# Two lists of loads and steps, and the last sum of an attention and feed-forward kernel, in a new order

## The chip, the cores and the metric

The kernel runs on one core of a Trainium2 chip. The metric is the device time of one execution in microseconds (us), the median of several runs. TensorE (PE) does the matmuls, ScalarE (ACT) and VectorE (DVE) the elementwise work, GpSimd (POOL) a little of it, and SyncE (SP) issues nearly all DMAs, one after the other, in an order that the program fixes.

## What is computed

The reference first does two small attentions between x (8 x 8 heads x 512 x 64) and a state (8 x 8 heads x 32 x 64), and feeds the joined result (4352 rows of 512) through a layer with a squared ReLU:

```python
xread = softmax(scale * x @ state.T) @ state
sread = softmax(scale * state @ x.T) @ x
rows = concatenate([xread, sread], axis=2)      # 8 x 8 heads x 544 x 64 -> 4352 x 512
h = maximum(rows @ w_in, 0.0)                   # d_ff = 2048
out = (h * h) @ w_out                           # 4352 x 512
```

## The kernel before, in words

The rows of `out` are worked on in nine blocks: blocks 0 to 7 hold the 512 rows that one batch entry's x reads make, block 8 the 256 rows of all state reads. Each f32 operand of a large matmul is split into a high and a low part in a faster format (`k_hi`, `k_lo`; `g_hi`, `g_lo`; the two halves of `w`), and three matmuls (high by high, high by low, low by high) stand for one. All matmuls of a block go through line 414 (`mm3`).

Rows @ w_in is not taken from the reads themselves: state @ w_in is made once per block ("W2", tile `w`) and multiplied by the softmax weights (`k_hi`, `k_lo`). For blocks 0 to 3 W2 is made on the spot (`w2ps`). For blocks 4 to 7 it is made beforehand by `quad_w2` (line 855), for four blocks at a time: ACT copies a piece of w_in (`q`, L860), DVE takes the low part (L863), PE multiplies (`qps`, L868), the result is copied out of PSUM (`qo`, L872) and SP writes it to HBM (`w_d`, L875). `load_w2` (L879) reads it back in four loads of 512 KB per block (tile `w2r`, L881), and `split_w2` splits each (ACT L887, DVE L890).

In the late blocks 4 to 8 the second product is done on pairs of d_ff slices, p = 0 to 7. For a pair, seven products of smaller matrices take the place of eight (the "fewer" tiles hold sums of w_out's quarters). A late block has two halves u: the first 256 rows are summed while the hidden slices are made, pair by pair, and the second 256 rows afterwards, in the order of `again_order`, which this text calls places 0 to 7. For a pair the ACT lines are 1086 (ReLU), 1087 (square of the first half's rows, into `ga`) and 1089 (square of the second half's rows, into `gb`). Most `gb` tiles are written to HBM at once (`g_d`, L1091), with their sums (`ge`, L1149), and read back later into `ga` and `gd` (L1094, L1104), since SBUF is full. A `gb` tile comes from a pool tag "g" with two buffers, one of which is held by a kept pair; so the next `gb` waits until the write of the last one has landed. The hidden slice is held in PSUM (tile `ph`, two buffers): PE can't start the slice after the next before ACT has read both squares out of it.

For each pair's operands ACT makes the high parts (L1138, L1142) and DVE the low parts (L1139, L1143). Even places use the tiles `k_hi` and `k_lo`, odd ones a tile `gs` from the tag "x", which has two buffers. The same tag holds `xn` (x by rows, loaded by `load_n`, L503) and `xp` (x cut into 32 x 32 pieces for a transpose on DVE, loaded by `load_p`, L519, four steps of four DMAs of 64 KB; the transposes are the steps `prep`, L544). The tag "wraw", also with two buffers, holds `w2r`, `eB` (exponentials on their way to HBM, written by the step `transposes` as `e_d`, L729) and `eT` (read back by `load_e`, L733, for the state read `sread`).

The order of all work is written out by hand as a list of words. A word is a step; a `~` in front runs it up to its next yield, so that its parts land between those of other steps. Each engine and SP keep exactly this order. The list for blocks 0 to 3 is the string `FIRST`; for the late blocks the function `late` builds it. In `late`, `a[p]` are the words after pair p in the first half of block b and `z[p]` those in the second half (`a[7]` stands at place 1 of the second half), n is block b + 1 and m is b + 2:

```python
        a[0] = "" if b == 4 else f"load_w2.{b}.2"
        a[1] += f" ~w2.{b}.4 w2.{b}.4 load_w2.{b}.3 "
            a[4] += f" {two} load_w2.{n}.0"
            a[7] += f" {two} ~w2.{n}.0 w2.{n}.0 load_w2.{n}.1"
                a[k + 1 + j // 2] += f" load_p.{m}.{j}"
```

Sums are accumulated in PSUM banks x, y, z and w (`acc_x` and so on), and read out by `step_sum` (L1152). At the end of block 8 pair 7 is summed with plain products: six matmuls of 512 columns into y, then six of 256 and three of 512 columns into w; DVE adds y and then w to the partial results in two halves each (L1209), and after each half SP stores it (L1214).

Of the kernel before, what the change touches and what calls it, by code (L numbers as in the profile page):

```python
# [97 lines left out]
    ~quad.0.1 ~accumulate.1.10 ~w2.0.4 ~hidden.1.15 ~transposes.3  # L98
    hidden.1.13 ~w2.0.4 w2.0.4 split_k.0.0 ~split_k.0.1 ~accumulate.1.13 load_p.4.3
    hidden.1.14 accumulate.1.13 split_k.0.1  # L100
    hidden.1.15 ~quad.0.2 ~quad.0.1 accumulate.1.10 accumulate.1.14 ~quad.0.2 ~hidden.0.8 ~hidden.0.8 quad.0.1
    accumulate.1.12
    hidden.0.8 ~quad.0.3 ~softmax.3.0 quad.0.2 ~quad.0.3 load_p.4.1 load_p.4.2 accumulate.1.15 ~hidden.0.9
    ~hidden.0.10 ~hidden.0.9 ~quad.0.3 accumulate.0.8 ~quad.0.3 ~quad.1.0
# [12 lines left out]
    ~sread.3 accumulate.3.0 ~quad_states.1 transposed_scores.4.0 ~exp_s.4.0  # L117
    hidden.3.1 ~hidden.3.2 ~quad_states.1 accumulate.3.1 load_p.5.0 transposed_scores.4.1 ~softmax.4.0 ~hidden.3.2
    ~quad_states.1
    hidden.3.2 ~softmax.4.1 ~exp_s.4.0 ~hidden.3.3 exp_s.4.0 quad_states.1 accumulate.3.2 ~hidden.3.3 ~exp_s.4.1  # L120
    hidden.3.3 ~exp_s.4.1 ~hidden.3.4 exp_s.4.1 ~quad.2.0 ~transposes.4 accumulate.3.3 ~hidden.3.4 ~softmax.4.1
    ~softmax.4.0 ~transposes.4
    hidden.3.4 transposes.4 ~hidden.3.5 ~quad.2.0 accumulate.3.4 ~hidden.3.5 spill_wi.1
    hidden.3.5 ~quad.2.0 ~softmax.4.0 ~hidden.3.6 accumulate.3.5 ~quad.2.0 sread.3 ~softmax.4.0 ~quad.2.1 quad.2.0
    ~hidden.3.6 ~hidden.3.7
    ~fewer.0 ~fewer.0
    hidden.3.6 load_p.5.1 spill_wi.2 ~w2.3.4 ~quad.2.1 load_p.5.3 ~w2.3.4 load_w2.4.0 accumulate.3.6 w2.3.4 ~hidden.3.7 ~quad.2.1
    hidden.3.7 fewer.0 ~hidden.3.8 ~quad.2.2 ~fewer.1 ~quad.2.2 accumulate.3.7 ~hidden.3.8 ~quad.2.1 ~softmax.4.1
    ~fewer.1 hidden.3.8 ~fewer.1 fewer.1 quad.2.1 ~hidden.3.9 ~softmax.4.0 ~softmax.4.0 ~quad.2.2 accumulate.3.8 ~quad.2.3 ~quad.2.2 ~hidden.3.9
    ~quad.2.3 quad.2.2 ~hidden.3.10  # L130
    hidden.3.9 load_p.5.2 ~softmax.4.0 ~quad.2.3 ~hidden.3.10 accumulate.3.9 ~quad.3.0
    hidden.3.10 ~fewer.2 ~fewer.2 ~fewer.2 ~quad.2.3 ~softmax.4.0 ~hidden.3.11 quad.2.3 ~w2.3.6 accumulate.3.10 ~w2.3.6 ~hidden.3.11 w2.3.6
    ~hidden.3.12
# [13 lines left out]
    return p < FEWER[blk][u]  # L147


def again_order(blk):  # L150
    n = FEWER[blk][1]
    if blk == 4:
        return [2, 3, 0, 1, 4, 5, 6, 7]
    return [p + k for p in range(n - 2, -1, -2) for k in (0, 1)] + [0] * (n % 2) + list(range(n, 8))


def late():

    w = []
    for b in (4, 5, 6, 7):  # L160
        n, m, last = b + 1, b + 2, b == 7
        ob = again_order(b)
        more = {u: [""] * 8 for u in range(2)}
        a, z = more[0], more[1]
        two = f"~softmax.{n}.0 ~softmax.{n}.1"
        k = 1
        a[0] = "" if b == 4 else f"load_w2.{b}.2"
        a[k] += f" scores.{n} ~sread.{b} ~sread.{b} "
        a[1] += f" ~w2.{b}.4 w2.{b}.4 load_w2.{b}.3 "
        if last:  # L170
            a[k] += f"~exp_s.{n}.0 ~exp_s.{n}.1 sread.{b} load_n.8.0"
        else:
            a[k] += f"transposed_scores.{n}.0 transposed_scores.{n}.1 ~exp_s.{n}.0 ~exp_s.{n}.1 sread.{b} start.{m}"
        a[k + 1] += f" ~exp_s.{n}.0 ~exp_s.{n}.1 exp_s.{n}.0 exp_s.{n}.1"
        a[3] += f" ~w2.{b}.6 w2.{b}.6"
        a[3 if last else 4] += f" ~transposes.{n} ~transposes.{n} transposes.{n}"
        if last:
            a[3] += " ~move_sread"
            a[4] = "load_e.8"
            z[1] = "~move_sread move_sread load_wi.0 ~sread.8 ~sread.8 sread.8 load_wi.1"  # L180
            z[3] = "~split_wi.0 split_wi.0 load_wi.2"
            z[5] = "~split_wi.1 split_wi.1"
        else:
            a[2] += f" {two}"
            a[3] += f" {two}"
            a[4] += f" {two} load_w2.{n}.0"
            a[5] += f" {two}"
            a[6] += f" {two}"
            a[7] += f" {two} ~w2.{n}.0 w2.{n}.0 load_w2.{n}.1"
            for j in range(4):  # L190
                a[k + 1 + j // 2] += f" load_p.{m}.{j}"
            z[2] += f" {two}"
            z[3] += f" ~softmax.{n}.0 softmax.{n}.0"
            z[4] += f" ~w2.{n}.2 w2.{n}.2 ~softmax.{n}.1 softmax.{n}.1"
            z[5] += f" prep.{m}.0 prep.{m}.1"
            z[6] += f" prep.{m}.2 prep.{m}.3 load_e.{n} load_n.{n}.0"
        if b == 4:
            a[1] += " load_f.4"
            a[4] = a[4].replace(" transposes.5", " load_f.5 transposes.5") + " ~fewer.4"
            a[5] += " fewer.4 ~fewer.5"  # L200
            a[6] += " ~fewer.5 ~fewer.5"
            z[0] += " fewer.5"
            z[7] += " ~fewer.6 ~fewer.6"
        if b == 5:
            a[0] += " fewer.6"
        before = "accumulate.3.15" if b == 4 else f"sum.{b - 1}.1.{again_order(b - 1)[7]}"
        chain = "~hidden.{b}.{f} ~hidden.{b}.{g} {pe} ~hidden.{b}.{f} hidden.{b}.{f} {few} ~hidden.{b}.{g} {few}"
        chain += " ~parts.{b}.0.{q} hidden.{b}.{g} parts.{b}.0.{q}"

        def hide(blk, q, pe):  # L210

            if blk == 8:
                t = "~hidden.{b}.{f} ~hidden.{b}.{g} {pe} hidden.{b}.{f} {few} "
                t += f"~split_wi.{q + 1} split_wi.{q + 1} load_wi.{q + 2} " if q else ""
                t += "hidden.{b}.{g} {few} {out} {few2} parts.{b}.0.{q}"
            else:
                t = chain
            few = "~parts.{b}.0.{q}".format(b=blk, q=q) if seven(blk, q, 0) else ""
            out = f"~sum.8.0.{q - 1}" if q == FEWER[8][0] else ""
            t = t.format(b=blk, f=2 * q, g=2 * q + 1, q=q, pe=pe, out=out, few=few, few2="~parts.{b}.0.{q}".format(b=blk, q=q))  # L220
            return t

        def load(blk, at):

            return f"load_g.{blk}.{ob[at]} load_d.{blk}.{ob[at]}"

        def again(q):

            few = f"~parts.{b}.1.{q} ~parts.{b}.1.{q}" if seven(b, q, 1) else ""
            return f"{few} parts.{b}.1.{q}"  # L230

        if b == 4:
            w += [hide(4, 0, "~" + before), before, "~w2.4.2 w2.4.2 load_w2.4.2"]
        for p in range(8):
            w += [load(b, 3).split()[0]] if p == 6 else []
            if p < 7:
                w += [hide(b, p + 1, f"~sum.{b}.0.{p} " + (before if p == 0 and b > 4 else ""))]
            else:
                w += [f"~sum.{b}.0.{p}", again(ob[0])]
                w += ["sum.{}.0.{}".format(b, 6)] if FEWER[b][0] > 6 else []  # L240
            w += [f"sum.{b}.0.{p}"] if p < (6 if FEWER[b][0] > 6 else 7) else []
            w += [{4: load(b, 2), 6: load(b, 3).split()[1], 7: load(b, 4)}[p]] if p in (4, 6, 7) else []
            w += [a[p]] if p < 7 else []
        for p in range(8):
            if p == 7:
                w += [f"~hidden.{n}.0 ~hidden.{n}.1"]
            w += [f"~sum.{b}.1.{ob[p]}"]
            if p == 1:
                w += [f"sum.{b}.0.7"]
            if p < 7:  # L250
                w += [again(ob[p + 1]), f"sum.{b}.1.{ob[p]}"]
            if p == 7:
                w += [hide(n, 0, "").replace(f"~hidden.{n}.0 ~hidden.{n}.1  ", "")]
            w += [a[7]] if p == 1 else []
            w += [load(b, k) for k in {0: (5, 6), 1: (7,)}.get(p, ())]
            w += [z[p]]
    for p in range(8):
        if p < 7:
            w += [hide(8, p + 1, f"~sum.8.0.{p} " + ("sum.7.1.7" if p == 0 else ""))]
        else:  # L260
            w += ["~sum.8.0.7"]
        w += [f"sum.8.0.{p}"]
    return " ".join(w)
# [35 lines left out]
def tile_attn_moe(  # L299
# [17 lines left out]
    B, H, S, D = x.shape  # L317
    Ns = state.shape[2]
    DM, DFF = w_in.shape
# [17 lines left out]
    V, A, T, SP, PL = nc.vector, nc.scalar, nc.tensor, nc.sync, nc.gpsimd  # L337
    traced, last = [0], {}
# [44 lines left out]
    def banks(name):  # L383

        return ps_b.tile([P, 2, S], F32, tag="psb", name=name)
# [766 lines left out]
    def step_sum(blk, u, p):  # L1152
# [22 lines left out]
        else:  # L1175
            for bank, ws in ((by, (a11, a12)), (bw, (a21, a22))):
                pairs = [(a, (wo[2 * p + k][:, 0], wo[2 * p + k][:, 1])) for k, a in enumerate(ws)]
                if at == n and bank is bw:
                    for h in range(2):
                        c = ts(h, DM // 2)  # L1180
                        mm3(bank[:, c], [(pairs[0][0], [r[:, c] for r in pairs[0][1]])], first=False, last=False)
                    pairs = pairs[1:]
                mm3(bank, pairs, first=False, last=end)
# [19 lines left out]
        if end:  # L1203
            n = P // B
            for i, o, bank in zip((1, 0), held.pop((blk, u, "o")), (by, bw)):
                o = o.rearrange("p h f -> p (h f)")
                halves = [slice(0, DM // 2), slice(DM // 2, DM)]
                for c in [slice(0, DM)] if blk < B else halves:
                    V.tensor_add(o[:, c], bank[:, c], o[:, c])  # L1209
                    if blk < B:  # L1210
                        SP.dma_start(out_v[blk, ts(2 * u + i, P)], o)
                    else:
# [300 lines left out]
```

## Time and profile before

| | us |
|---|---|
| median of 3 runs (640.1 to 641.74) | 641.44 |
| the profiled execution | 639.41 |
| its span, first to last instruction | 637.6 |
| PE busy | 626.7 (98%) |
| DVE busy | 496.5 (78%) |
| ACT busy | 431.3 (68%) |
| POOL busy | 26.2 (4%) |

PE is the engine to look at: 98% of the span it has a matmul in flight. The granted clock is 0.999 of full speed (2.4 GHz) over the span. In the trace the late block 4 lies at about 332 to 393 us, block 5 at 393 to 457, block 6 to 522, block 7 to 587, block 8 to the end. A time in a row of the timeline is the start of the instruction from the span's start; the second number is how long it took, or for a row with a count the time from the first one's start to the last one's end; in brackets stands how long the engine was idle before it, and what ended that.

### The profile page before, as it was taken

How to read it: one execution, taken by the hardware profiler on the slowest of the kernel's cores; microseconds unless marked ns; L12 is line 12 of the kernel's file. 1: busy time of each engine (PE TensorE's matmuls, PEld its weight loads, DVE VectorE, ACT ScalarE, POOL GpSimd, SP SyncE). 2: the span in 40 equal slices, each digit the busy share in tenths (PEclk: the TensorE clock that was granted, in tenths of full speed). 3: DMA queues.
4: the chain of work that ended last, by engine and by line, in shares of the span. 5: the costliest groups of instructions: out<-in, count | busy, mean ns of one | idle time of the engine just before them, and what ended most of it. 6: DMA issues, size and time to landing. Idle time of an engine off the chain costs nothing.

```text
span 637.6 us, 11600 instructions
## 1 busy us (share of the span) xinstructions
PE 626.7 (98%) x4296; PEld 518.6 (81%) x4296; DVE 496.5 (78%) x1001; ACT 431.3 (68%) x813; POOL 26.2 (4%) x37
## 2 busy tenths in 40 slices
PE   7999999999999999999999999999999999999997
PEld 6577777777787777777888788899989998999996
DVE  5999767574676888868987797999769976865996
ACT  5987658754765565778896775777667766875452
POOL 1210000000000000000000202000200020001000
PEclk9999999999999999999999999999999999999999
DMA  8983948450422777196376895669465857694421
GB/s 315 370 189 119 280 104 233 118 132 2 115 87 66 225 191 213 19 213 181 87 229 208 202 233 174 193 153 258 154 217 131 229 175 213 175 269 145 127 73 34
DMA packets 155561, 109.22 MB, mean 171 GB/s; under 512 B 104560, under 2 KB 126576, under 8 KB 155504
## 3 DMA queue, kind: packets, MB, share of 16 engines
q1 hardware_dynamic: 154688, 108.08, 59.6%
q8 instruction: 34, 0.56, 0.4%
q10 hardware_dynamic: 816, 0.39, 0.2%
q14 instruction: 23, 0.19, 0.1%
HBM read 66.83 MB, written 41.62 MB: 170 GB/s over the span
## 4 chain that ended last, share of the span: by engine, by line
PE 84%; ACT 6%; DMA 4%; DVE 4%; issue 1%; SPq 0%; DVEq 0%; ACTq 0%
PE acc L414 25%; PE ph L414 24%; PE acc_x L414 6%; PE acc_z L414 6%; PE acc_yw L414 6%; PE acc_y L414 4%; PE w2ps L426 3%; PE acc_w L414 3%; PE ph L1223 2%; DMA g_d<-gb 2%; PE qps L868 2%; PE pr L745 1%; PE sc L426 1%; PE ph L1224 1%; DMA w2r<-w_d 1%; DMA xn<-in_x_dram 1%
## 5 line engine op out<-in xcount | busy, mean ns | idle before, releaser
L414 PE MATMUL ph<-k_hi,w 128*128 128x512 f32 x504 | 171.8, 395 | 1.6 <-ACT gb L1089 1.6
L414 PE MATMUL acc<-wo,g_hi 128*128 128x512 f32 x512 | 159.3, 392 | 0.1
L414 PEld LDWEIGHTS ph<-k_hi,w 128*128 128x128 f32 x504 | 94.6, 188 | 31.9 <-issue 8.0
L414 PEld LDWEIGHTS acc<-wo,g_hi 128*128 128x128 f32 x512 | 95.5, 188 | 24.7 <-issue 3.3
L414 PE MATMUL acc<-wo,g_lo 128*128 128x512 f32 x256 | 100.1, 391 | 0.4 <-DVE g_lo L998 0.4
L414 PE MATMUL ph<-k_lo,w 128*128 128x512 f32 x252 | 98.3, 390 | 0.0
L998 DVE TENSOR_TENSOR g_lo<-ph,g_hi 128x512 fp32r<-128x512 f32 x64 | 43.7, 685 | 35.6 <-ACT g_hi L407 34.8
L414 PEld LDWEIGHTS acc<-wo,g_lo 128*128 128x128 f32 x256 | 48.0, 188 | 11.9 <-DVE g_lo L998 1.7
L990 ACT ACTIVATE ph<-ph 128x512 f32<-128x512 f32 x59 | 34.6, 587 | 32.2 <-PE ph L414 31.4
L414 PEld LDWEIGHTS ph<-k_lo,w 128*128 128x128 f32 x252 | 47.4, 188 | 8.4
L1086 ACT ACTIVATE ph<-ph 128x512 f32<-128x512 f32 x64 | 37.7, 589 | 19.9 <-PE ph L414 18.3
L991 ACT ACTIVATE ph<-ph 128x512 f32<-128x512 f32 x59 | 34.3, 582 | 1.9
L407 ACT CAST g_hi<-ph 128x512 fp32r<-128x512 f32 x53 | 31.1, 587 | 5.7 <-PE acc L414 2.8
L1138 ACT CAST gs<-ga 128x384 fp32r<-128x384 f32 (+1 forms) x32 | 17.5, 545 | 21.2 <-PE acc_yw L414 13.8
L1138 ACT CAST k_hi<-ga 128x384 fp32r<-128x384 f32 (+1 forms) x40 | 20.9, 522 | 13.2 <-DVE ga L1232 12.7
L1143 DVE TENSOR_TENSOR k_lo<-gd,k_hi 128x512 fp32r<-128x512 f32 x36 | 24.8, 688 | 4.6 <-ACT k_hi L1142 4.6
L1087 ACT ACTIVATE ga<-ph 128x256 f32<-128x256 f32 x64 | 24.6, 385 | 2.0
L1190 POOL TENSOR_TENSOR o_x<-o_x 128x256 f32<-128x256 f32 x5 | 4.7, 930 | 517.2 <-DMA xp<-in_x_dram 300.9
L829 DVE TENSOR_TENSOR w<-w2ps,w 128x512 fp32r<-128x512 f32 (+1 forms) x34 | 20.1, 633 | 7.3 <-ACT w L407 7.3
L407 ACT CAST w<-w2ps 128x512 fp32r<-128x512 f32 (+1 forms) x26 | 13.6, 567 | 17.3 <-DVE w L405 10.3
L1139 DVE TENSOR_TENSOR k_lo<-ga,k_hi 128x384 fp32r<-128x384 f32 (+1 forms) x40 | 22.3, 559 | 3.8 <-ACT k_hi L1138 3.8
L890 DVE TENSOR_TENSOR w<-w2r,w 128x1024 fp32r<-128x1024 f32 x16 | 19.5, 1220 | 6.8 <-ACT w L887 6.7
(236 smaller groups left out, 1380.0 us busy)
## 6 DMA issues: line engine op xcount, KB each, us to landing
w_d<-qo SPq DMA_DIRECT2D x32, 256.0 KB, 2.6
w2r<-w_d SPq DMA_DIRECT2D x16, 512.0 KB, 4.5
wo_raw<-in_moe_w_out_dram SPq DMA_DIRECT2D x16, 511.8 KB, 8.0
wi_raw<-in_moe_w_in_dram SPq DMA_DIRECT2D x16, 511.5 KB, 6.3
xp<-in_x_dram SPq DMA_DIRECT2D x112, 64.0 KB, 2.5
g_d<-gb SPq DMA_DIRECT2D x24, 256.0 KB, 3.3
ga<-g_d SPq DMA_DIRECT2D x24, 256.0 KB, 5.0
g_d<-ge SPq DMA_DIRECT2D x19, 256.0 KB, 2.6
```

Source lines behind the costliest of these rows:

```text
L407: A.copy(out, src)
L414: T.matmul(ps, l, r, start=first and i == 0, stop=last and i == len(seq) - 1)
L426: T.matmul(ps, l, r, start=True, stop=True)
L829: V.tensor_sub(w[:, u, g, 1], ps[g], w[:, u, g, 0].bitcast(F32))
L990: A.activation(ph, ph, AF.Relu)
L991: A.activation(ph, ph, AF.Square)
L998: V.tensor_sub(glo, ph, ghi.bitcast(F32))
L1086: A.activation(ph, ph, AF.Relu)
L1087: A.activation(raws[blk, 0, p][:, 2 * k : 2 * k + 2].rearrange("p i t -> p (i t)"), ph[:, : 2 * P], AF.Square)
L1138: A.copy(hi[:, r], raw[:, r])
L1139: V.tensor_sub(lo[:, r], raw[:, r], hi[:, r].bitcast(F32))
L1143: V.tensor_sub(lo[:, 4:], d, hi[:, 4:].bitcast(F32))
```

## The change

1. `FIRST`, block 1: the rest of `quad.0.1` (copying out of PSUM, DVE L872, and its two writes) goes ahead of `~quad.0.2` (the low part of the next piece, DVE L863) and of two parts of `hidden.0.8`.
2. `FIRST`, block 3: the first part of `exp_s.4.1` (DVE reduce L628 and a small multiply, L630) goes behind the end of `hidden.3.3` (DVE `g_lo`, L998); the first part of `quad.2.0` (ACT copies, L860) goes behind the end of `hidden.3.4`; `load_w2.4.0` is issued after `quad.2.2` and not after `load_p.5.3`.
3. `late`: the first W2 load of block n moves from `a[4]` to `a[3]`, the second from `a[7]` to `a[5]`, the third from `a[0]` of block n to `z[4]` of the block before. The loads of x move from `a[2]` and `a[3]` to `z[2]` and `z[3]`.
4. `step_sum`, block 8: the last sum into w is made as two halves of six matmuls of 256 columns, each half in a bank of its own (`tail` is the second); y's result is added and stored whole, w's in two halves. There are three last stores in place of four.

```diff
-    hidden.1.15 ~quad.0.2 ~quad.0.1 accumulate.1.10 accumulate.1.14 ~quad.0.2 ~hidden.0.8 ~hidden.0.8 quad.0.1
+    hidden.1.15 ~quad.0.2 ~quad.0.1 accumulate.1.10 accumulate.1.14 quad.0.1 ~quad.0.2 ~hidden.0.8 ~hidden.0.8
...
-    hidden.3.2 ~softmax.4.1 ~exp_s.4.0 ~hidden.3.3 exp_s.4.0 quad_states.1 accumulate.3.2 ~hidden.3.3 ~exp_s.4.1
-    hidden.3.3 ~exp_s.4.1 ~hidden.3.4 exp_s.4.1 ~quad.2.0 ~transposes.4 accumulate.3.3 ~hidden.3.4 ~softmax.4.1
+    hidden.3.2 ~softmax.4.1 ~exp_s.4.0 ~hidden.3.3 exp_s.4.0 quad_states.1 accumulate.3.2 ~hidden.3.3
+    hidden.3.3 ~exp_s.4.1 ~exp_s.4.1 ~hidden.3.4 exp_s.4.1 ~transposes.4 accumulate.3.3 ~hidden.3.4 ~softmax.4.1
     ~softmax.4.0 ~transposes.4
-    hidden.3.4 transposes.4 ~hidden.3.5 ~quad.2.0 accumulate.3.4 ~hidden.3.5 spill_wi.1
+    hidden.3.4 ~quad.2.0 transposes.4 ~hidden.3.5 ~quad.2.0 accumulate.3.4 ~hidden.3.5 spill_wi.1
...
-    hidden.3.6 load_p.5.1 spill_wi.2 ~w2.3.4 ~quad.2.1 load_p.5.3 ~w2.3.4 load_w2.4.0 accumulate.3.6 w2.3.4 ~hidden.3.7 ~quad.2.1
+    hidden.3.6 load_p.5.1 spill_wi.2 ~w2.3.4 ~quad.2.1 load_p.5.3 ~w2.3.4 accumulate.3.6 w2.3.4 ~hidden.3.7 ~quad.2.1
...
-    ~quad.2.3 quad.2.2 ~hidden.3.10
+    ~quad.2.3 quad.2.2 load_w2.4.0 ~hidden.3.10
...
+XP = 2, 2, 3, 3
...
-        a[0] = "" if b == 4 else f"load_w2.{b}.2"
+        a[0] = ""
...
-            a[3] += f" {two}"
-            a[4] += f" {two} load_w2.{n}.0"
-            a[5] += f" {two}"
+            a[3] += f" {two} load_w2.{n}.0"
+            a[4] += f" {two}"
+            a[5] += f" {two} load_w2.{n}.1"
             a[6] += f" {two}"
-            a[7] += f" {two} ~w2.{n}.0 w2.{n}.0 load_w2.{n}.1"
-            for j in range(4):
-                a[k + 1 + j // 2] += f" load_p.{m}.{j}"
+            a[7] += f" {two} ~w2.{n}.0 w2.{n}.0"
+            for j, at in enumerate(XP):
+                z[at] += f" load_p.{m}.{j}"
...
-            z[4] += f" ~w2.{n}.2 w2.{n}.2 ~softmax.{n}.1 softmax.{n}.1"
+            z[4] += f" ~w2.{n}.2 w2.{n}.2 ~softmax.{n}.1 softmax.{n}.1 load_w2.{n}.2"
...
+                if blk == B and end and bank is bw:
+                    for h, half in enumerate((bw, tail := banks("acc8_0_v")[:, 0])):
+                        c = ts(h, DM // 2)
+                        mm3(half[:, c], [(a, [r[:, c] for r in rs]) for a, rs in pairs], first=h == 1, last=True)
+                    continue
...
-                for c in [slice(0, DM)] if blk < B else halves:
-                    V.tensor_add(o[:, c], bank[:, c], o[:, c])
+                for c in [slice(0, DM)] if blk < B or i else halves:
+                    V.tensor_add(o[:, c], (tail if c.start else bank)[:, c], o[:, c])
```

## Rows read from the trace of the kernel before

**Rows 1.** Page: engine totals; costliest groups (busy, mean ns, idle before).

```profile
PE 626.7 (98%) x4296; PEld 518.6 (81%) x4296; DVE 496.5 (78%) x1001; ACT 431.3 (68%) x813; POOL 26.2 (4%) x37
...
L414 PE MATMUL acc<-wo,g_hi 128*128 128x512 f32 x512 | 159.3, 392 | 0.1
```

**Rows 2.** Timeline of PE, block 4 (start us, us, instruction, idle before).

```profile
362.58 1.52 PE L414 MATMUL acc_w<-wo,gs 128*128 128x512 f32 x6
365.55 0.50 PE L414 MATMUL ph<-k_hi,w 128*128 128x512 f32 x1 [1.45 <-ACT gb L1089]
...
367.39 0.50 PE L414 MATMUL ph<-k_hi,w 128*128 128x512 f32 x1 [0.17 <-ACT gb L1089]
```

**Rows 3.** Timeline of ACT, block 4.

```profile
359.26 0.38 ACT L1089 ACTIVATE gb<-ph 128x256 f32<-128x256 f32 x1
...
365.11 0.38 ACT L1089 ACTIVATE gb<-ph 128x256 f32<-128x256 f32 x1 [3.53 <-DMA g_d<-gb]
```

**Rows 4.** Timeline of SP, block 4.

```profile
356.98 4.20 SPq L519 DMA_DIRECT2D xp<-in_x_dram  x8
```

**Rows 5.** DMAs issued at 361.28, 407.58, 409.68, 337.99: KB, us to landing.

```profile
g_d<-gb SPq DMA_DIRECT2D x1, 256.0 KB, 3.7
...
w2r<-w_d SPq DMA_DIRECT2D x1, 512.0 KB, 3.7
...
g_d<-gb SPq DMA_DIRECT2D x1, 256.0 KB, 2.3
...
g_d<-gb SPq DMA_DIRECT2D x1, 256.0 KB, 5.4
```

**Rows 6.** Timeline of PE, last place of block 4.

```profile
389.62 0.62 PE L414 MATMUL acc_yw<-wo,k_hi 128*128 128x512 f32 x2
390.29 0.50 PE L414 MATMUL acc_yw<-wo,k_lo 128*128 128x512 f32 x1
```

**Rows 7.** Timeline of ACT, second half of block 4.

```profile
386.72 1.05 ACT L887 CAST w<-w2r 128x1024 fp32r<-128x1024 f32 x1 [0.80 <-DMA w2r<-w_d]
```

**Rows 8.** DMAs issued at 434.29 and 437.75 (block 5): KB, us to landing.

```profile
e_d<-eB SPq DMA_DIRECT2D x1, 128.0 KB, 4.7
...
gd<-g_d SPq DMA_DIRECT2D x1, 256.0 KB, 4.6
```

**Rows 9.** Timeline of PE, place 3 of block 5's second half.

```profile
447.30 0.52 PE L414 MATMUL acc_x<-wo,gs 128*128 128x256 f32 x3
```

**Rows 10.** Block 5 windows: us; PE, PEld, DVE, ACT, POOL busy; PEclk, DMA share, GB/s.

```profile
420.30:424.40 4.10, 4.10 (x25) 3.58 (x25) 3.85 (x12) 3.98 (x9) 0.00 (x0) 1.00 0.74 154
444.00:457.30 13.30, 13.30 (x115) 13.30 (x114) 12.78 (x22) 7.83 (x14) 0.96 (x1) 1.00 0.52 183
```

**Rows 11.** Timeline of DVE, second half of block 5.

```profile
456.66 1.29 DVE L544 STREAM_TRANSPOSE xT<-xp 128x512 f32<-128x512 f32 x2
459.87 0.29 DVE L1111 TENSOR_TENSOR gd<-ga 128x128 f32<-128x128 f32 x1 [1.92 <-ACT ga L1087]
```

**Rows 12.** Timeline of DVE, end of block 8.

```profile
633.27 0.76 DVE L1209 TENSOR_TENSOR o_z<-acc_w,o_z 128x256 f32<-128x256 f32 x2 [0.65 <-PE acc_w L414]
```

**Rows 13.** Timeline of SP, end of block 8.

```profile
633.72 1.19 SPq L1214 DMA_DIRECT2D out_dram<-o_z  x2
```

**Rows 14.** Timeline of DVE, block 3.

```profile
264.72 0.68 DVE L628 TENSOR_REDUCE m<-sc 128x1 f32<-128x512 f32 x1
...
265.51 0.69 DVE L998 TENSOR_TENSOR g_lo<-ph,g_hi 128x512 fp32r<-128x512 f32 x1
...
269.27 0.69 DVE L998 TENSOR_TENSOR g_lo<-ph,g_hi 128x512 fp32r<-128x512 f32 x1
```

**Rows 15.** Timeline of PE, block 3.

```profile
266.26 0.50 PE L414 MATMUL acc<-wo,g_lo 128*128 128x512 f32 x1 [0.39 <-DVE g_lo L998]
...
270.51 0.39 PE L414 MATMUL acc<-wo,g_lo 128*128 128x512 f32 x1
```

**Rows 16.** Timeline of PE, block 1.

```profile
204.61 1.16 PE L868 MATMUL qps<-q,s 128*128 128x512 f32 x4 [0.22 <-DVE qo L872]
```

## The prediction, made before the result was known

> **What bounds the kernel now.** I read the page's totals first: PE is busy 626.7 us of a span of 637.6 [rows 1], so at most 10.9 us can come from PE's waits, unless matmuls are made fewer. Then I read PE's timeline stretch by stretch for the waits, because the share says nothing of their places, and from each wait I went to the timeline of the engine that ended it, and from there to SP's. Two prices are needed. A matmul of 512 columns that follows another takes (1.52 - 0.392) / 5 = 0.226 us of PE's pace: six take 1.52 [rows 2], and one alone is 0.392 from start to end [rows 1]. The difference, 0.17 us, is the end of a matmul that the next one normally overlaps. So a wait that shows as a gap g costs g + 0.17, and as the first matmul after a gap shows 0.50 in place of 0.39 [rows 1, 2], 0.11 more.
>
> **Loads of x out of the first half (change 3).** In block 4 PE waits 1.45 us before a hidden slice, and soon after 0.17 us more, both times for ACT's `gb` [rows 2]. They cost 1.45 + 0.17 + 0.17 + 0.17 + 2 x 0.11 = 2.18 us. ACT itself waited 3.53 us for the landing of the last `gb` [rows 3]: that tile was complete at 359.26 + 0.38 = 359.64, but SP was handing out eight loads of x from 356.98 to 361.18 [rows 4], so its write went out only at 361.28 and landed 3.7 us later, at 365.0 [rows 5]. With the x loads gone from `a[2]` and `a[3]` the write goes out at about 359.7. The two nearest landings are 2.3 and 3.7 us [rows 5], so it lands at 362.0 to 363.4, and the next `gb` is done by 363.8. PE wants it at 362.58 + 6 x 0.226 = 363.94 [rows 2]. Both waits go: -2.18 us. If something else holds the write as long, nothing goes (the second rival). The other late blocks show no such wait, so this gain comes once.
>
> **W2's loads earlier (change 3).** At the end of block 4 a matmul starts at 390.29 where the pair ahead of it allows 389.62 + 2 x 0.226 = 390.07 [rows 6]: 0.22 + 0.11 = 0.33 us. The chain behind it is the split of W2: ACT waited 0.80 us for `w2r` [rows 7], and DVE's low parts slipped with it. The load moves from `a[7]` to `a[5]`, ahead of the reloads of places 3 to 6, so the wait on ACT goes: -0.33, at worst 0. The two moves together: -2.5, between -2.5 and 0.
>
> The move adds a wait on SP. At `a[5]` the load needs a "wraw" buffer that holds `eB` until the last of the four `e_d` writes, issued just ahead in `a[4]`, has landed: 434.29 + 4.7 = 439.0 in block 5 [rows 8]. Queued behind it on SP are the reloads of `ga` and `gd` for place 3, the last `gb` write, and then all other reloads. The `gd` that went out at 437.75 [rows 8] would go out at about 439.0 + 3 x 0.5 = 440.5 (each issue takes about 4.20 / 8 = 0.53 [rows 4]) and land 4.6 us later, at 445.1. Place 3's sum starts at 447.30 [rows 9]; the third product is the first to take the `gd` tile, at 447.30 + 6 x 0.117 = 448.0; a high and a low part come before, at most 0.7 each by the low part of block 3 [rows 14], so the data is wanted at 446.6. That leaves 1.5 us, so I cost the wait at nothing; with the cover gone ACT would wait for `gd` and PE lose what exceeds 1.5. `load_w2.n.2` at `z[4]` takes a buffer that was free since `a[7]`, and nothing urgent stands behind it.
>
> **The x loads in their new place.** `z[2]` and `z[3]` stand behind place 2's and 3's sums. Seven products of three 256-column matmuls, (0.52 - 0.17) / 3 = 0.117 us each [rows 9], make a place 21 x 0.117 = 2.5 us, so in block 5 the issue begins near 447.3 - 2.5 = 444.8 at the earliest. Sixteen issues take 16 x 0.53 = 8.4 us, to 453.2; with a landing of 2.3 to 5.4 [rows 5] the last is in at 455.5 to 458.6. The DMA engines give about the same: eight x loads kept them busy 0.74 of 4.1 us [rows 10], so sixteen need 6.1 us; from 444.0 to 457.3 they were busy 0.52 x 13.3 = 6.9 us without x [rows 10], and 444 + 6.9 + 6.1 = 457.0. DVE takes the last transposes at 456.66 and 457.31, and then waits 1.92 us anyway [rows 11]. So the last x data may come as late as 457.3 + 1.9 = 459.2 before it costs anything: 0.6 to 3.7 us of slack, cost 0. This is the thinnest cover in the change.
>
> **The tail (change 4).** After the last matmul DVE now makes two adds (0.76 us for both, and the first store follows the first), and SP two store issues, 1.19 / 2 = 0.6 apart [rows 12, 13]. The new order leaves one add and one store behind the last matmul: -0.60. In exchange three matmuls of 512 columns become six of 256: 6 x 0.117 - 3 x 0.226 = +0.02. Sum -0.58. Bounds: -0.65, and -0.3 if the store that is now larger delays the last one.
>
> **Block 3 (change 2).** A matmul waits 0.39 us for `g_lo` [rows 15], which DVE makes only after a reduce of 0.68 us [rows 14]. With the reduce moved behind, PE gains 0.39 + 0.17 + 0.11 = 0.67. But the reduce begins a chain (maximum, exponential, product) and now starts some 0.6 later; the next `g_lo` then moves from 269.27 to about 269.9 and ends near 270.6 [rows 14], while PE, now 0.67 earlier, wants it at 270.51 - 0.67 = 269.84 [rows 15]. PE would wait until 270.65, or 0.8, + 0.11: net about +0.2. Bounds: -0.67 if the next `g_lo` slips ahead of the chain, +0.35 if it ends 0.15 later. I take +0.2.
>
> **Block 1 (change 1).** PE waits 0.22 us for `qo` before `qps` [rows 16]. The swap puts those copies ahead of a low part that the same group of matmuls also needs, so one delay takes the other's place: 0. Bounds -0.22 - 0.17 - 0.11 = -0.5, and +0.1. The later `load_w2.4.0` costs 0: its split is many steps further on.
>
> **The sum** is -2.5 - 0.58 + 0.2 + 0 = -2.9 us. The profiled execution took 639.41, 2.0 under the median of the runs; the same 2.9 us off each makes 636.5 profiled and 641.44 - 2.9 = 638.5 as the time.
>
> **Rivals.** *A stays (640.7, chance 0.14).* The W2 load now stands at `a[3]`, ahead of the `gb` write that mattered. The one `gb` write that went out right behind a W2 load took 5.4 us to land, and one 2.1 us behind another W2 load took 2.3 [rows 5]. With 5.4 the write lands at 359.7 + 5.4 = 365.1, as now, and the 2.18 us stay: 638.5 + 2.2 = 640.7. Against it: several pairs' work lies between that load and the write. The Trainium skill ("DMA: Bandwidth & Descriptors", section "Queues, rings and completion order") says that each DMA engine takes descriptors in the order of its ring and that the completion count lands only after that engine's earlier writes; by that rule a write right behind a 512 KB load waits for it. The 5.4 agrees with it, the 2.3 shows that two microseconds between them are enough.
>
> *x too late (646.0, chance 0.12).* If the tag "x" gives a buffer only two places later (place 3's `gs` taking the free one), the issue starts 5.0 us later and x is in at 460.5 to 463.6, which is 1.3 to 4.4 past 459.2, some 2.5 in the middle. DVE keeps its order, so the first steps of the next block wait with it, in blocks 4, 5 and 6: 3 x 2.5 = 7.5, and 638.5 + 7.5 = 646.0, slower. It decides at 459.2 in block 5. For it speaks that the reloads fill the DMA engines just there; against it, that place 1's `gs` is free before `z[2]`.
>
> *x a little late (640.2, chance 0.08).* The wait at `a[5]` pushes all reloads by its 440.5 - 437.75 = 2.75 us, and the x data behind them on the DMA engines comes at 457.0 + 2.75 = 459.75, 0.55 past the point: 3 x 0.55 = 1.7, and 640.2.
>
> *More is won (637.1, chance 0.12).* Block 3's next `g_lo` slips through (-0.67 in place of +0.2) and block 1's 0.5 is recovered: 638.5 - 0.9 - 0.5 = 637.1.
>
> *The loads aren't earlier (638.9, within the forecast).* If W2's load at `a[5]` waits past the reloads' own time, only the 0.33 is lost.
>
> **How the numbers follow.** The forecast has the remaining 0.54, the last case included, with an own spread of 637.5 to 639.9. 0.3%, about what a measurement of this kernel can tell from no change, is 1.9 us: faster means under 639.5, slower over 643.4. Faster: 0.48 of the forecast and the 0.12 of more won, 0.60. Same: the forecast's other 0.06, 0.14 and 0.08, 0.28. Slower: 0.12. The range goes from all terms at their good bounds (-2.5 - 0.65 - 0.67 - 0.5 = -4.3, with 0.3 for small slips of low parts: 636.8) to the first rival with the tail and block 3 at their bad bounds (640.7 + 0.3 + 0.15 + 0.1 = 641.3); outside is the 0.12 and a little more.
>
> **What would show it.** In the new profile PE's waits near 365 and 390 should be gone, with ACT's `gb` no longer ended by a DMA; a new PE wait for `g_lo` some 4 us behind the place of the old one in block 3; x loads on SP right behind the last reload in the second halves; DVE's last transposes still followed by an idle time; one store after the last add. DVE transposes that a landing of `xp` releases, with no idle time after, would make the slower case; a `gb` ended by a landing in block 4's fifth pair the first rival; ACT waiting for `gd` at place 3 would say that the wait at `a[5]` is not covered.

## The result, and the profile after

| | before | after |
|---|---|---|
| median, 6 runs each (us) | 642.74 (640.1 to 645.36) | 637.11 (636.45 to 638.43) |
| ratio, with 95% interval | | 0.9914 (0.9885 to 0.9944) |
| the profiled execution, and its span | 639.41, 637.6 | 637.1, 634.5 |

The kernel became faster by 0.6 to 1.2%; 638.5 was forecast for a median of 641.44, a gain of 2.9 us. The two profiled executions differ by 3.1 us in the span, the medians by 5.6. The kernel before took 641.44 in the three executions that the forecast knew and 642.74 in six, which is 1.3 of the 5.6; the time after is 1.4 under the forecast's 638.5. So there are two questions: does each edit do in the two profiles what the steps said, and where do the other 2 us or so come from, which these two profiles don't hold?

For the first I lined up the lists of matmuls of the two traces and took the difference of their starts. It changes at a few places only:

| place (start in the trace before, us) | forecast | difference gained there |
|---|---|---|
| the first 60 us, no edit there | 0 | -0.40 |
| block 1, `qps` (204.6) [rows 16] | 0 | -0.46 |
| block 3, first and second `g_lo` (266.3, 270.5) [rows 15] | +0.2 | -0.76 + 0.94 = +0.18 |
| block 4, hidden slice after `gb` (365.5 to 367.7) [rows 2] | -2.18 | -2.19 |
| block 4, a new wait (372.1) | 0 | +0.42 |
| block 4, last place (390.3) [rows 6] | -0.33 | -0.32 |
| small steps elsewhere | 0 | -0.25 |
| last matmul and tail [rows 12, 13] | -0.58 | +0.07 - 0.14 = -0.07 |

Their sum is -3.1. PE's timeline of the kernel after, at these places (start, us, instruction; in brackets the idle time before and what ended it):

```profile
203.83 1.08 PE L871 MATMUL qps<-q,s 128*128 128x512 f32 x4
...
264.81 0.39 PE L417 MATMUL acc<-wo,g_lo 128*128 128x512 f32 x1
...
269.72 0.50 PE L417 MATMUL acc<-wo,g_lo 128*128 128x512 f32 x1 [0.67 <-DVE g_lo L1001]
...
363.21 0.39 PE L417 MATMUL ph<-k_hi,w 128*128 128x512 f32 x1
...
369.57 1.20 PE L417 MATMUL acc_y<-wo,gs 128*128 128x512 f32 x4 [0.31 <-DVE gs L1142]
...
387.38 0.39 PE L417 MATMUL acc_yw<-wo,k_lo 128*128 128x512 f32 x1
```

Three waits of before are gone (at `qps`, at the first `g_lo` and at the hidden slice), and at the last place of block 4 the matmul at 387.38 follows the pair ahead of it at full pace; in block 3 a wait stands at the second `g_lo`, as forecast; and one at 369.57 is new. SP's timeline shows why the hidden slice starts at once: nothing stands ahead of the `gb` write.

```profile
356.24 0.42 SPq L884 DMA_DIRECT2D w2r<-w_d  x1
358.39 0.32 SPq L1094 DMA_DIRECT2D g_d<-gb  x1
...
380.23 10.25 SPq L522 DMA_DIRECT2D xp<-in_x_dram  x16
```

The write went out at 358.39 and landed 2.1 us later; the W2 load ahead of it took 3.6 (the profile's DMA issues: KB each, us to landing):

```profile
g_d<-gb SPq DMA_DIRECT2D x1, 256.0 KB, 2.1
```

The x loads, 16 from 380.23 on, have used up DVE's idle time. DVE's timeline, ends of blocks 5 and 6:

```profile
457.85 0.71 DVE L547 STREAM_TRANSPOSE xT<-xp 128x512 f32<-128x512 f32 x1 [1.14 <-DMA xp<-in_x_dram]
458.48 0.25 DVE L1114 TENSOR_TENSOR gd<-ga 128x128 f32<-128x128 f32 x1
...
524.02 0.71 DVE L547 STREAM_TRANSPOSE xT<-xp 128x512 f32<-128x512 f32 x1 [2.41 <-DMA xp<-in_x_dram]
524.65 0.25 DVE L1114 TENSOR_TENSOR gd<-ga 128x128 f32<-128x128 f32 x1
```

The transposes now wait for landings, and the 1.92 us of idle time behind them [rows 11] is gone. PE has no wait there yet.

### The profile page after: what moved, and what is told of

It reads as the page before. It is cut to its first block, busy times and chain, and to the rows that moved or that the text cites. A ratio compares the mean times of both kernels' runs of the same rounds, so it can differ in the third digit from the quotient of the medians.

```text
span 634.5 us, 11623 instructions
## 1 busy us (share of the span) xinstructions
PE 625.3 (99%) x4299; PEld 519.0 (82%) x4299; DVE 498.0 (78%) x1000; ACT 431.5 (68%) x813; POOL 26.1 (4%) x37
## 4 chain that ended last, share of the span: by engine, by line
PE 90%; DVE 4%; ACT 3%; DMA 2%; issue 1%; SPq 0%; ACTq 0%; DVEq 0%
PE acc L417 27%; PE ph L417 25%; PE acc_yw L417 7%; PE acc_x L417 6%; PE acc_z L417 6%; PE acc_y L417 4%; PE acc_w L417 3%; PE w2ps L429 3%; PE qps L871 2%; PE ph L1231 2%; PE pr L748 1%; PE sc L429 1%; PE ph L1232 1%; DMA wi_raw<-in_moe_w_in_dram 1%; DMA f<-wo_d 1%; PE ph L974 1%
## 5 line engine op out<-in xcount | busy, mean ns | idle before, releaser
L547 DVE STREAM_TRANSPOSE xT<-xp 128x512 f32<-128x512 f32 x28 | 19.1, 698 | 10.1 <-DMA xp<-in_x_dram 9.8
L1145 ACT CAST k_hi<-gd 128x512 fp32r<-128x512 f32 x36 | 22.3, 620 | 5.7 <-DVE gd L1118 4.7
```

Of the source, the lines that this page charges most:

```text
L1145: A.copy(hi[:, 4:], d)
```

## The experiments

Each kernel is the whole change with the edit shown, unless said otherwise. Times are medians; where only one execution was made, it is said. A ratio is to the kernel before, timed beside it.

**The whole change again.**

> The whole change once more, timed in five rounds beside the kernel before. Theory 1 (what the two profiles show, matmul by matmul): the sum of the moved waits is 0.4 in block 1, -0.2 in block 3, 2.2 in block 4, 0.1 at the end, about 2.5 us, and 0.5 more in the first 12 us that belongs to no edit; the ratio should be about 0.996 (2.5 / 641). Theory 2: the medians are right (637.11 against 642.74), the gain is about 5.5 us, ratio 0.991, and half of it lies in something that one pair of profiles does not show. The ends of the two differ by 3 us.

Measured: 637.62 against 642.46 for the kernel before, ratio 0.9932 (0.9911 to 0.9954). The interval leaves out 0.996 and, just, 0.991. With the first result's 0.9914 (0.9885 to 0.9944) the gain is 4.4 to 5.5 us, more than the two profiles hold: theory 1 falls, and theory 2's half that they don't show is to be looked for.

**x's loads back in the first half (W2's loads stay early).**

```diff
-            for j, at in enumerate(XP):
-                z[at] += f" load_p.{m}.{j}"
+            for j in range(4):
+                a[k + 1 + j // 2] += f" load_p.{m}.{j}"
```

> The whole change, but x's loads again in the first half of the late blocks. Theory 1: the write of gb waits behind eight x loads on SP again, PE's waits of 1.45 and 0.17 us in block 4 come back (2.18 with the drains); the new wait of 0.47 us some 5 us later goes, since PE comes there later; so 1.7 us slower than the whole change. DVE's last transposes no longer wait for x. Theory 2 (the W2 load ahead of the write is what matters, not x): no wait comes back, within 0.3 us of the whole change.

Measured: 641.92, ratio to before 0.998 (0.996 to 1.0001); 4.3 us slower than the whole change, where 1.7 was expected. PE, ACT and SP in block 4:

```profile
366.44 0.50 PE L417 MATMUL ph<-k_hi,w 128*128 128x512 f32 x1 [2.74 <-ACT gb L1092]
...
366.00 0.38 ACT L1092 ACTIVATE gb<-ph 128x256 f32<-128x256 f32 x1 [4.86 <-DMA g_d<-gb]
...
357.04 6.55 SPq L522 DMA_DIRECT2D xp<-in_x_dram  x8
363.69 0.43 SPq L1094 DMA_DIRECT2D g_d<-gb  x1
```

The wait is back, by the mechanism named: the write stands behind eight x loads. Here they took SP 6.55 us in place of 4.20 [rows 4], and PE waited 2.74 in place of 1.45 [rows 2]. Theory 2 falls; the size of the wait is what theory 1 had wrong. Matmul by matmul it costs 3.5 us more than in the whole change, and two late low parts in blocks 6 and 7 (513.9 and 585.2) cost about 0.6 and 1.1. The W2 load, now at `a[3]`, went out at 356.57, right ahead of these eight x loads, where the kernel before had none; two of their issues took 1.82 and 1.54 us. So in this order W2's move seems to lengthen the `gb` wait, though no run shows that it is the reason.

**W2's loads back in their old places (x's stay in the second half).** This was run twice, first for one execution, then for ten.

```diff
-            a[3] += f" {two} load_w2.{n}.0"
-            a[5] += f" {two} load_w2.{n}.1"
+            a[4] += f" {two} load_w2.{n}.0"
+            a[7] += f" {two} ~w2.{n}.0 w2.{n}.0 load_w2.{n}.1"
...
+        a[0] = "" if b == 4 else f"load_w2.{b}.2"
```

> The whole change, but W2's loads in their old places; x's loads stay in the second half. Theory 1: the 2.18 us of block 4 stay away; the 0.33 us at the last place of block 4 come back, as ACT waits for the W2 landing again; and since a W2 load of 512 KB now stands right ahead of x's, x's data comes some 1.4 us later, which exceeds what is left in block 6 (about 1 us), a few tenths there. Sum +0.3 to +0.8 us. Theory 2 (W2's place matters only through the landing of gb): block 4's end as in the whole change, 0.

Measured: 643.19 in one execution, where 0.3 to 0.8 us over the whole change's 637.1 was expected. PE and ACT at the last place of block 4, and the landing of the W2 load issued at 379.35:

```profile
389.38 0.91 PE L417 MATMUL acc_yw<-wo,k_hi 128*128 128x512 f32 x2 [1.98 <-ACT k_hi L1141]
391.34 0.80 PE L417 MATMUL acc_yw<-wo,k_lo 128*128 128x512 f32 x1 [1.05 <-DVE k_lo L1142]
...
387.24 1.04 ACT L890 CAST w<-w2r 128x1024 fp32r<-128x1024 f32 x1 [3.50 <-DMA w2r<-w_d]
...
w2r<-w_d SPq DMA_DIRECT2D x1, 512.0 KB, 7.9
```

The load lands at 387.2, where the profile before had it at 386.7 (379.9 + 6.8); over this kernel's two profiles and three of the kernel before it is always 386.7 to 387.4. So the landing goes by what is queued in the DMA engines (100% busy from 380 to 386, below), not by when PE wants it. PE has come 2.2 us earlier, because the `gb` wait is gone, and pays it back here. And the clock falls, here at 389.8, between the two waits (busy time by stretch; us, PE, PEld, DVE, ACT, POOL, granted clock, DMA share, GB/s):

```profile
380.00:386.00 6.00, 6.00 (x53) 6.00 (x52) 4.44 (x8) 2.62 (x5) 0.00 (x0) 1.00 1.00 328
386.00:389.40 3.40, 1.42 (x13) 1.22 (x12) 1.08 (x1) 2.16 (x4) 0.00 (x0) 1.00 0.94 124
389.80:390.30 0.50, 0.48 (x2) 0.00 (x0) 0.50 (x2) 0.50 (x3) 0.41 (x1) 0.50 0.82 133
392.00:396.00 4.00, 4.00 (x14) 3.43 (x13) 2.16 (x4) 0.00 (x0) 1.98 (x3) 0.50 0.80 144
398.00:410.00 12.00, 12.00 (x66) 10.41 (x65) 9.50 (x26) 8.00 (x20) 0.00 (x0) 1.00 0.65 177
```

> The whole change with W2's loads in their old places, timed in three rounds. In its one look it took 643.19: PE waited 2.0 and 1.05 us at the last place of block 4 for parts behind the W2 landing, and then ran at half the clock. Theory 1: x's loads in the second half make this a steady loss; all runs 641 to 644, ratio to the kernel before about 1.0, some 0.7 to 0.9% slower than the whole change. Theory 2: it was one unlucky landing; the median is within 0.3% of the whole change (637 to 639.5).

Measured: 642.91 (640.99 to 645.66), ratio to before 0.9995 (0.997 to 1.0019). The whole change wasn't timed beside it; by the two ratios that it has (0.9914 and 0.9932) it is 0.6 to 0.8% faster. That is theory 1, though two of the ten runs took longer than its 644. The profiled execution shows the same two waits, at 2.32 and 1.23 us:

```profile
389.56 0.73 PE L417 MATMUL acc_yw<-wo,k_hi 128*128 128x512 f32 x2 [2.32 <-ACT k_hi L1141]
391.52 0.63 PE L417 MATMUL acc_yw<-wo,k_lo 128*128 128x512 f32 x1 [1.23 <-DVE k_lo L1142]
```

So neither move alone, with the small edits of blocks 1, 3 and 8 beside it, is worth anything that can be told from no change (0.998 and 0.9995), and the two together are worth nearly all of the 0.7 to 0.9%. (The small edits without either move weren't run.)

**The kernel before, profiled twice more.**

> The kernel before, profiled and timed again. The spans of its other runs go from 638.7 to 644.5 us, median about 640.4; the profile that the forecast was read from had 637.6. Theory 1 (the waits of this kernel for DMA landings vary, and the first profile was one of the short ones): this profile's span is 639 to 644, its PE wait for gb in block 4 is longer than 1.45 us, or W2's wait at the end of block 4 is longer than the 0.05 us shown (with a stretch at the lower TensorE clock behind it, if the granted clock is 0.993 to 0.998), or a low part in blocks 5 to 7 comes late; these make up the 1.5 to 6 us. Theory 2 (the surplus lies outside of the matmuls, at start and end): the same waits as in the first profile, and the surplus in the first 20 us.

> The kernel before once more, one look, for a third set of its waits. Theory 1: a span of 639 to 644 and another mix of the same waits (gb in block 4; W2 at the end of block 4; a low part in a second half). Theory 2: the waits of the first profile to within 0.3 us.

Measured: the first of these had a span of 638.7, the second 639.9. The ten executions of the first kernel spanned 638.7 to 644.8; the profile that the forecast was read from, with 637.6, is under all of them; of 23 more executions of that kernel one had 637.5. Its `gb` waits are the same in all three profiles (1.45, 1.44 and 1.40 us). What differs is the rest. In the second of the two, PE and ACT at the end of block 4:

```profile
391.29 0.50 PE L414 MATMUL acc_yw<-wo,k_lo 128*128 128x512 f32 x1 [1.24 <-DVE k_lo L1139]
...
387.19 1.05 ACT L887 CAST w<-w2r 128x1024 fp32r<-128x1024 f32 x1 [1.52 <-DMA w2r<-w_d]
```

The W2 wait there is 1.24 us where the forecast's profile has a gap too short for a bracket [rows 6]; with drain and restart it cost 1.5. Matmul by matmul, this execution and the profile after are 5.3 us apart at the end: 2.2 at `gb`, 1.6 at the W2 wait, 0.8 at a low part in block 7 (585.1), 0.5 in block 1, 0.2 for the other steps together. Theory 1 of both holds in its kind: the waits for landings differ from execution to execution. Two of its places are wrong, though: the `gb` wait hardly moved, and in the first of the two the surplus came from block 3:

```profile
294.52 1.21 PE L868 MATMUL qps<-q,s 128*128 128x512 f32 x4 [0.70 <-ACT qo L872]
```

That place and block 7's low part also appear, or don't, in kernels with the change (0.60 us at `qo` in the last kernel below), so they are no gain of it.

**Blocks 0 to 3 in their old order.** The edit is the list `FIRST` of the kernel before.

> The whole change, but blocks 0 to 3 in their old order. Theory 1 (from the two profiles): PE's wait for qo in block 1 is back, +0.46 us there; in block 3 the wait moves back from the second to the first g_lo, -0.2 us. Theory 2 (the forecast, both neighbours are needed anyway): block 1 within 0.1 us of the whole change.

Measured (one execution): 637.73. PE at the two places:

```profile
204.45 0.93 PE L871 MATMUL qps<-q,s 128*128 128x512 f32 x3 [0.22 <-DVE qo L875]
...
266.00 0.50 PE L417 MATMUL acc<-wo,g_lo 128*128 128x512 f32 x1 [0.36 <-DVE g_lo L1001]
```

Lined up with the whole change, +0.47 at `qps` and -0.32 over block 3. Theory 1 (a late low part in block 7 is in this execution too, 0.44 us in the gap).

**x's loads one and two places later.**

```diff
-XP = 2, 2, 3, 3
+XP = 3, 3, 4, 4
```

> The whole change with x's loads one place later (third and fourth in place of second and third), about 2.5 us. In the whole change DVE's last transpose of x already begins late by the 1.9 us that it had to spare, or more. Theory 1: behind DVE there is more cover: the low part that follows is ready 3.1 us early for PE in block 4, 2.8 in block 5, 1.2 in block 6; so 2.5 us later costs nothing in blocks 4 and 5 and about 1.3 us in block 6. Theory 2 (the forecast's rule, late past the idle time of DVE costs PE as much in every block): about 2.5 in each of three blocks, 7.5 us.

Measured (one execution): 636.04, span 634.2; no wait of PE is added anywhere. But this tests neither theory, since the edit moves nothing: SP has no other work between the old and the new words, and all engines ran the same instructions in the same order as in the whole change. SP of this kernel, block 4:

```profile
379.67 11.55 SPq L522 DMA_DIRECT2D xp<-in_x_dram  x16
391.32 0.43 SPq L884 DMA_DIRECT2D w2r<-w_d  x1
```

The last x landed at 392.9, 457.4 and 521.5 in blocks 4 to 6, where the first profile of the whole change has 392.5, 457.7 and 523.8. So this is one more execution of the whole change. With `XP = 4, 4, 5, 5` a W2 load goes ahead of the last eight x loads, and the last x does land later, by 2.8, 3.9 and 2.6 us (5.0 was meant):

> The whole change with x's loads two places later, about 5.0 us. Theory 1: 5.0 less the cover of 3.1, 2.8 and 1.2 us: 1.9 + 2.2 + 3.8, about 8 us. Theory 2 (late past DVE's idle time costs as much): about 15 us. Theory 3 (the landings catch up, as the reloads are over by then): under 4 us.

Measured (one execution): 638.28, span 636.5, 1.5 to 2 us more than the whole change's two profiles. 1.4 of it is one wait, not where any theory put it, but in the first half of block 5 (PE, and DVE ahead of it):

```profile
404.82 0.39 PE L417 MATMUL acc_x<-wo,gs 128*128 128x256 f32 x1 [0.94 <-DVE gs L1142]
...
402.69 0.68 DVE L1217 TENSOR_TENSOR o_z<-acc_yw,o_z 128x512 f32<-128x512 f32 x1
...
404.22 0.55 DVE L1142 TENSOR_TENSOR gs<-ga,gs 128x384 fp32r<-128x384 f32 x1
```

DVE carries the delay from block 4's end through some ten us of its list before PE meets it. Theory 3 has the size (under 4 us), with landings that were less late than meant. In the first halves of blocks 6 and 7 PE doesn't meet it at all; DVE's list there lacks the sums of w_out's pieces (L1029 to L1038) that it has in block 5, which may be why.

**The waits that the change left or made.** In block 3 `g_lo` goes one product and one transpose further up:

```diff
-    ~softmax.4.0 ~transposes.4
-    hidden.3.4 ~quad.2.0 transposes.4
+    hidden.3.4 ~softmax.4.0 ~transposes.4
+    ~quad.2.0 transposes.4
```

> The whole change with one more step moved in block 3: the second g_lo ahead of a product and a transpose on DVE. Theory 1: the wait that the change moved from the first g_lo to the second (0.67 us in the gap, 0.83 with the drain) is only DVE's order; it goes, -0.8 us, and nothing takes its place. Theory 2: the softmax chain that is now later makes the next wait; the sum stays within 0.2 us.

Measured (one execution): 636.34, span 634.5. The wait of 0.67 is gone (-0.93 against the whole change), and 25 us on a part of it is back, +0.41:

```profile
294.78 0.73 PE L417 MATMUL acc<-wo,g_hi 128*128 128x512 f32 x2 [0.40 <-ACT g_hi L410]
```

Theory 1 for the place; the sum is between the two, and a low part in block 7 is late in this execution, by 0.52 us (579.66). And for the new wait in block 4:

```diff
-            a[5] += " fewer.4 ~fewer.5"
-            a[6] += " ~fewer.5 ~fewer.5"
+            a[5] += " fewer.4"
+            a[6] += " ~fewer.5 ~fewer.5 ~fewer.5"
```

> The whole change with the first sums of w_out's pieces for pair 5 (DVE, waiting for the landing of f) moved one step later, behind the low part that PE wants. Theory 1: PE's new wait of 0.31 us in block 4 (0.47 with the drain) is DVE's wait for f ahead of that low part; it goes, -0.47 us. Theory 2: DVE is the limit there, and another low part becomes late; 0.

Measured (one execution): 637.01. The wait at 369.6 is gone, -0.62, and another low part is late 3 us on, +0.6 (`k_lo`, 0.24 us in the gap): theory 2. The wait itself is not steady either: the second profile of the whole change doesn't have it.

**A version that goes further**: `g_lo` first, x one place later (which, as above, moves nothing), and y's last store issued by ACT.

```diff
-                        SP.dma_start(rows[:, :, c], o[:, c])
+                        (A if i else SP).dma_start(rows[:, :, c], o[:, c])
```

> The whole change with three more steps: the second g_lo of block 3 ahead of a product and a transpose; x's loads one place later; and y's last store issued by ACT in place of SP. Theory 1: -0.9 in block 3, of which 0.4 comes back some 25 us later; 0 for x; and at the end SP has two stores to issue in place of three, so the last one starts when its add is done and not 0.3 later: -0.3. Sum -0.8 us against the whole change, ratio to the kernel before about 0.992. Theory 2: the store on ACT costs what it frees (its issue on ACT or a later landing), and block 3's gain comes back whole: within 0.2 us of the whole change.

Measured: 636.9, ratio to before 0.9897 (0.9862 to 0.9932); the whole change has 0.9932 (0.9911 to 0.9954). The intervals overlap, so it isn't shown to be faster. In its profile the 0.9 of block 3 is gone and 1.3 is back at 293 to 296. And 0.9 us is lost in block 5's first half, at the place where two places later cost 1.4 (DVE, then PE):

```profile
394.25 0.71 DVE L547 STREAM_TRANSPOSE xT<-xp 128x512 f32<-128x512 f32 x1 [2.60 <-DMA xp<-in_x_dram]
...
403.75 0.39 PE L417 MATMUL acc_x<-wo,gs 128*128 128x256 f32 x1 [0.47 <-DVE gs L1142]
```

x is in the whole change's place here; its last part landed at 394.2, not 392.5 to 393.8, and DVE worked on with hardly a gap until that low part was done at 403.70. The tail (SP and ACT of this kernel, then the landing of its last store):

```profile
630.84 1.30 SPq L1222 DMA_DIRECT2D out_dram<-o_z  x2
...
630.45 0.64 ACTq L1222 DMA_DIRECT2D out_dram<-o_x  x1
...
out_dram<-o_z SPq DMA_DIRECT2D x1, 128.0 KB, 2.8
```

From the last matmul's end to the start of the last store's issue it is 631.55 - 631.06 = 0.49 us, against 631.04 - 630.28 = 0.76 in the whole change. But the store landed after 2.8 us in place of 2.5, and the span ended 4.4 us after the last matmul in place of 4.2: theory 2 for the tail.

## Why the prediction was right, and where it was not

**The `gb` wait, its mechanism and price**: right in the profile (2.18 forecast, 2.19 found), and shown by putting the x loads back (2.74 us of PE's wait for `gb`). Its rival, a write that lands late behind the W2 load, fell: 2.1 us after that load's issue the write took 2.1 us. The rule of the Trainium skill ("DMA: Bandwidth & Descriptors", section "Queues, rings and completion order") is not contradicted, since 512 KB ahead had two microseconds to leave; this write right behind such a load wasn't tried. Elsewhere one was: a `gb` write 0.8 us behind the W2 load at 369.44 of the trace before took 5.6 us.

**W2's wait**: the place and cause are right, the term was mis-sized. The forecast read 0.33 off one execution. In another execution of the same kernel it is 1.5, and with the `gb` wait away it would have been 3 to 4 us and half the clock after it. The step that failed is the one that added the two moves as if each were worth its own wait. They are in series: W2's landing is fixed by the DMA backlog, and each microsecond won at `gb` is lost at W2 unless W2 moves too; and with W2 moved alone the `gb` wait grew from 1.45 to 2.74. The sum came near only because the change makes both moves at once, and in part by luck: in the two profiles the tail fell 0.5 short and a new wait cost 0.42, while 0.46 in block 1, 0.40 in the first 60 us, where nothing was edited, and 0.25 of small steps came on top. The median after, 637.11, is the figure of the rival "more is won", but not by its way: block 3's low part didn't slip through.

**"The same 2.9 us off each"**: wrong, and here the other 2 us or so are. The profiled execution was 2.0 under the median, and I treated the 2.0 as a constant. They are, at least in part, waits that vary, and a change that takes loads out of the crowd can remove these as well: after, the profiled execution and the median agree within 0.1 us (0.6 in the second set). How the rest is shared isn't settled. In the ten timed executions of the kernel before, four had a mean granted clock of 0.995 to 0.997 and took 644.0 to 646.7 us, the six others, at 0.999 or more, took 641.0 to 642.6 (of 23 more beside them, one at 0.997 took 640.8); the twelve of the whole change lie at 0.998 or above. That the clock falls at the W2 waits is shown in the kernel with only x moved; that it was the same wait in those four executions is only argued, as no profile caught one, and the W2 wait of 1.24 in the third profile before came without a fall. With x's loads back, six of ten executions had 0.997 too, so the longer `gb` wait may do it as well; the profiled one, with 2.74, shows no fall.

**x's cover**: "cost 0" was right in the profiles of the whole change, the terms and the point at which it decides were not. The 16 issues took 10 to 12 us in place of 8.4. I put the point at 459.2 in block 5, which is 456.3 after the 2.9 us of earlier starts; the last data was used from 457.85, 1.5 later, and PE lost nothing. So the sign that I had named for the slow case, transposes released by a landing with no idle time behind them, came without its cost. Idle time on DVE was only the first layer of cover; the second is how far ahead of PE its low parts are. That layer is thin in block 5's first half: the low part at 403 was ready 1.0, 0.5 and 0.7 us before PE took it in the three profiles of the whole change's order (the kernel one place later counted in), and late in the last kernel. The slow rival's mechanism is real, at 0.9 to 1.4 us in one block; its price of 2.5 us in each of three was far too high.

**The wait at `a[5]`**: cost 0 was right, the cover was not as I had it. SP waited there until 372.0, when the last `e_d` write landed. The reloads behind it do hold ACT, by up to 3.0 us at place 3 of block 5, which is the sign that I had named for a wait that isn't covered:

```profile
440.56 0.51 ACT L1141 CAST gs<-ga 128x384 fp32r<-128x384 f32 x1 [2.95 <-DMA ga<-g_d]
442.58 0.63 ACT L1145 CAST gs<-gd 128x512 fp32r<-128x512 f32 x1 [1.51 <-DMA gd<-g_d]
```

The low part made from that `gd` was done at 444.13, and PE took it from 444.95 on without a wait: 0.8 us of cover was left.

**Block 3**: right, +0.18 for +0.2, and undone again by putting the old list back. **Block 1**: wrong, -0.46 for 0, though within its bounds. I counted the swap as one for one. But the two copies (1.28 us) went ahead of two low parts (1.40), and `qps` needs only the first of these to start:

```profile
201.35 1.28 DVE L875 COPY qo<-qps 128x512 f32<-128x512 f32 x2
202.66 1.40 DVE L866 TENSOR_TENSOR q<-wi,q 64x512 fp32r<-64x512 f32 x2
```

The first low part ends at 203.34, the second at 204.06, and `qps` goes at 203.83 without a wait.

**The tail**: wrong, -0.07 for -0.58. I took one issue off behind the last matmul and forgot that SP's three issues are a chain of their own, which begins with y's store: y is now added whole, its store goes out later, and each store waits for the issue ahead of it (SP after):

```profile
629.65 0.62 SPq L1222 DMA_DIRECT2D out_dram<-o_x  x1
630.36 1.23 SPq L1222 DMA_DIRECT2D out_dram<-o_z  x2
```

The last issue starts at 631.04, 0.76 after the last matmul's end, where it was 1.08 [rows 13]. Of this 0.32 the landing (+0.11), the end of the span behind it (+0.07) and the split of the matmuls (+0.07) took most back. Even the weak bound I had named, -0.3, was too good.

## What to carry to other kernels

Before pricing a wait for a landing, ask how it varies: a profiled execution well under the median of its kernel has short waits, and the difference to the median is part of what a change may win. Two waits for landings that follow each other on a bound engine are not a sum: removing the first moves the engine up against the second, so undo and redo each alone, and expect the pair to be worth more than its parts. And a wait that a reordering removes from an engine in strict order usually turns up one or two steps on; count it only after looking at what is late next. Last, look in the trace whether an edit to such a list has moved anything before reading a result from it: one here hadn't.

## What the runs showed of the hardware

In the first run with W2's loads in their old places, PE was busy 1.42 us of the 3.40 from 386.0, and had two waits of 1.98 and 1.05 us up to 391.3. The granted clock was 0.50 of full speed, which is the 1.2 GHz level, from 389.8, just behind the first wait, to 396.6, with PE busy all of it from 391.3; then it was 1.00 again. In the 4.0 us from 392 PE started 14 matmuls. So 3 us of waiting cost 6: lined up with the whole change, that execution lost 2.2 and 1.4 us at the two gaps and 2.5 more at the lower pace. In the second run, with waits of 2.32 and 1.23 us, the clock fell only behind the second, and for 3.4 us (391.7 to 395.2).

A 512 KB load of the late blocks landed in 3.4 to 4.7 us in the profile after, and in 6.8 to 8.3 from its old place at the end of block 4 (five profiles), with the DMA engines 94 to 100% busy in the one shown. The Trainium skill ("DMA: Bandwidth & Descriptors", section "Latency and other measured facts") says that a DMA's fixed cost rises with the load on HBM; no run here shows that by itself. When the load that took 7.9 us went out, seven transfers of 256 KB were still on their way; with its own 512 KB they take 7.2 us at the 328 GB/s of that stretch (an estimate), so the backlog of bytes ahead explains most of it.
